# Issuing the decay rows of each head pair from another engine's queue

## The chip, the cores and the metric

The program runs on one core of one Trainium2 chip. The metric is the device time of one execution in microseconds. A core has five engines that matter here: TensorE (PE, matrix products), VectorE (DVE), ScalarE (ACT), GpSimd (POOL) and SyncE (SP). Each works through a queue of its own in a fixed order, and an instruction that waits holds back everything behind it in that queue. DMA transfers are started from a queue (here SP's or POOL's) and then run beside the engines.

## The reference

Causal attention with forget gates, then a dense layer with squared ReLU, then a mixture of eight experts of which each token takes two. The attention, cut to its core (4 batches, 8 heads, 576 positions, head size 64):

```python
scores = scale * np.matmul(q, k.transpose(0, 1, 3, 2))
log_f = np.log(np.clip(f, 0.0001, 1.0))
cum = np.cumsum(log_f, axis=-1)
decay = cum[:, :, :, None] - cum[:, :, None, :]
scores = np.where(causal, -1000000000.0, scores + decay)
attn = np.exp(scores - max); attn /= attn.sum + 1e-09
x = attn @ v                       # 2304 tokens x 512
x = np.maximum(x @ w_in, 0) ** 2 @ w_out
out = sum over a token's top-2 experts e of weight * relu(x @ w1[e]) @ w2[e]
```

## The kernel before, in words

All products run on PE in half precision, each operand split into a high and a low half, so a product is three matmuls.

Attention of the first 256 query rows of each batch ("head" part) runs first. The remaining 320 rows are 48 *units* (b, i, p): batch b, block of 128 queries i = 2, 3, 4, head pair p. `att_tick` (from L801) takes the units one after the other and mixes them with the steps of the dense layer. The stations of a unit:

- `att_s` (L213 to L230) makes its scores on PE in two PSUM tiles `ps`.
- `att_exp` (L242 to L252): DVE takes the row maximum, ACT the exponential.
- `att_split` (L265 to L278): ACT and DVE split the result into two halves (`phl`, or `ph4` for i = 4), and one DMA transpose issued on SP brings it into `pt`.
- `att_pv` (L307, L310), three ticks later: PE multiplies `pt` with the values `vs` into `po`.

Between them PE has the dense layer: `mm1` (L483, tile `m1`, 12 matmuls of 384 columns) and `mm2` (L527, tiles `acc`, 9 matmuls of 512 columns).

The decay needs no product of its own. `prep(b, p)` loads keys and queries of a pair into `setk<p>` and `setq<p>` (KK, QQ): ACT copies at L184 and L185, DVE's low halves at L186 and L187, and then L189 copies six rows of the cumulative log gates, kept in the tile `c16`, by DMA into partitions 64 to 69 of KK's plane 0. The matmuls L214 and L226, 70 partitions deep, read them there. L189 waits for L186, which still reads that plane. `prep(b+1, p)` belongs to the tick of the unit (b, 4, p), so the four copies of a batch are written ahead of the batch's first scores. Behind L189 in SP's queue stand the load of the next pair (L90), weight loads (L455) and the transposes of the units (L267, L278).

POOL has little to do in this stage: small memsets of `ph4` (L272) and of zeros (L585), and the six scatters of each routed chunk (L668, `table`), which wait for DVE's `si` (L665).

The order on every engine is set by a scheduler that, while the program is built, plays the program forward with its own estimates of durations, and puts each instruction where it becomes ready in that play. The source fixes which work exists and what depends on what; it doesn't fix the place of a matmul on PE.

Of the kernel before, what the change touches and what calls it, by code (L numbers as in the profile page):

```python
# [18 lines left out]
B, H, S, D = 4, 8, 576, 64  # L19
# [33 lines left out]
def attn_moe_moe_kernel(ctx: ExitStack, tc, qka, qk, v, f, w_io, wgn, noise, w1, w2, out):  # L53
    nc = tc.nc
# [24 lines left out]
    c16 = apool.tile([96, S], F16, name="c16")  # L79
# [82 lines left out]
    KK, QQ, VS = {}, {}, {}  # L162

    def make_set(n):
        KK[n] = apool.tile([128, 2, 2, S], F16, name=f"setk{n}", tag=f"setk{n}", bufs=1)
        QQ[n] = apool.tile([128, 2, 2, REST], F16, name=f"setq{n}", tag=f"setq{n}", bufs=1)
        q2 = QQ[n][64:70, 1]
        nc.gpsimd.memset(q2, -8.0)
        nc.gpsimd.affine_select(q2[:, 0], q2[:, 0], [[0, REST]], ALU.is_ge, 0.0, base=2, channel_multiplier=-1)
        nc.gpsimd.affine_select(q2[:, 1], q2[:, 1], [[0, REST]], ALU.is_ge, 0.0, base=-3, channel_multiplier=1)  # L170
# [6 lines left out]
    def prep(b, p):  # L177
        n = p
        if b == 0:
            make_set(n)  # L180
        t = raw.pop(("qk", b, p))
        k_ = t[:, 0:2 * S].rearrange("p (z s) -> p z s", z=2)
        q_ = t[:, 2 * S:SK].rearrange("p (z s) -> p z s", z=2)
        nc.scalar.activation(KK[n][:, 0], k_, AF.Copy)  # L184
        nc.scalar.activation(QQ[n][:, 0], q_, AF.Copy, scale=-1.0)  # L185
        nc.vector.scalar_tensor_tensor(KK[n][:, 1], KK[n][:, 0], half, k_, op0=ALU.mult, op1=ALU.subtract)  # L186
        nc.vector.tensor_tensor(QQ[n][0:64, 1], q_[0:64], QQ[n][0:64, 0], op=ALU.add)  # L187
        h0 = 8 * b + 2 * p
        nc.sync.dma_start(KK[n][64:70, 0], c16[3 * h0:3 * h0 + 6, None, :].to_broadcast([6, 2, S]))  # L189

    def prep_v(b, p):
        v_ = raw.pop(("v", b, p))
# [608 lines left out]
    def att_tick(k, pool_of):  # L801
        if k == 0:
            prep(0, 0)
            prep_v(0, 0)
            load_qk(0, 2)
            load_v(0, 2)
        if k < 3:
            prep(0, k + 1)
            prep_v(0, k + 1)
            if k == 0:  # L810
                load_qk(0, 3)
                load_v(0, 3)
            elif k == 1:
                load_qk(1, 0)
        if k < NU:
            u = units[k]
            att_s(u, pool_of(k))
            att_exp(u)
            b, i, p = u
            if i == 4 and b + 1 < B:  # L820
                prep(b + 1, p)
                if p < 3:
                    load_qk(b + 1, p + 1)
                elif b + 2 < B:
                    load_qk(b + 2, 0)
                if p > 1:
                    load_v(b + 1, p - 2)
            if i == NB and b:
                prep_v(b, p)
                if p < 2:  # L830
                    load_v(b, p + 2)
# [225 lines left out]
```

## Time and profile before

| | |
|---|---|
| median of 3 runs | 1033.73 us (1032.12 to 1035.33) |
| the profiled execution's own time | 1035.69 us |
| its span, first to last instruction | 1034.0 us |
| PE busy | 948.4 us, 92% of the span |
| DVE, ACT, POOL busy | 57%, 44%, 18% of the span |
| mean granted clock of TensorE | 0.959 of full speed |

A busy share is an average over stages. The units run from about 100 to 520 us, the experts fill the time from about 580 us to the end. What an edit in the attention is worth is read from the idle time of PE in that stretch and from what ended it.

### The profile page before, as it was taken

Reading aid. Unit: us, or ns where it says so; the run is one execution under the profiler, and the core shown is the slowest. Engines: PE = TensorE matmul, PEld = TensorE weight load, DVE = VectorE, ACT = ScalarE, POOL = GpSimd, SP = SyncE. Lnnn points to the kernel's source line nnn. Section 1 sums busy time; section 2 is a strip of 40 time slices with the busy share of each in tenths; the row PEclk is TensorE's granted clock in tenths of the full one; section 3 lists DMA queues with packets and bytes.
Section 4 is the critical chain, followed back from the end, with each engine's and each line's share of the span. In section 5 each row is a group of like instructions: output and inputs, shape, how many; then the busy total and the mean of one; then the engine's idle time right before and its main releaser. Section 6 shows DMA issues by size and latency. Waiting matters only on the chain.

```text
span 1034.0 us, 17720 instructions
## 1 busy us (share of the span) xinstructions
PE 948.4 (92%) x6850; PEld 534.5 (52%) x6850; DVE 590.5 (57%) x1325; ACT 456.4 (44%) x1005; POOL 181.5 (18%) x202
## 2 busy tenths in 40 slices
PE   2667899999889998999999899999899999999996
PEld 1554455455445554555544444466556565656562
DVE  7978989947668776776568242254534343432221
ACT  3875776756647655755455120134423232321010
POOL 8000000002020011002000404333231313120202
PEclk9558999999899998999999999999999999999999
DMA  7889898874977957973387542559994748350303
GB/s 257 243 197 247 221 237 210 209 188 64 196 146 180 255 134 108 200 134 72 62 255 240 127 98 27 97 75 291 293 192 116 196 118 229 82 122 2 51 3 49
DMA packets 240681, 160.92 MB, mean 156 GB/s; under 512 B 194163, under 2 KB 204915, under 8 KB 240595
## 3 DMA queue, kind: packets, MB, share of 16 engines
q1 hardware_dynamic: 230482, 138.75, 55.4%
q0 software_dynamic: 10112, 21.02, 10.7%
q8 instruction: 54, 0.88, 0.4%
q14 instruction: 33, 0.26, 0.1%
HBM read 88.97 MB, written 24.30 MB: 110 GB/s over the span
## 4 chain that ended last, share of the span: by engine, by line
PE 59%; DMA 10%; DVE 2%; issue 2%; SPq 1%; ACT 1%; POOL 1%; POOLq 0%; DVEq 0%
PE e L780 19%; PE e L767 17%; PE m L483 9%; PE acc L527 9%; DMA pt<-phl 4%; DMA wr<-in_w_dram 3%; PE po L307 1%; PE po L310 1%; DMA pt<-ph 1%; DMA xg<-x2d,tix 1%; PE ps L213 1%; PE ps L214 1%; DMA xgT<-xg 1%; DVE w2s L704 1%; DMA out_dram<-y,tix 0%
## 5 line engine op out<-in xcount | busy, mean ns | idle before, releaser
L767 PE MATMUL e<-xgT,w1s 128*128 128x320 f16 (+2 forms) x1536 | 218.1, 303 | 8.4 <-DMA xgT<-xg 4.6
L483 PE MATMUL m<-xT,win 128*128 128x384 f16 x1152 | 208.9, 331 | 4.8 <-ACT r L487 2.8
L780 PE MATMUL e<-w2s,hT 128*128 128x512 f16 x960 | 211.2, 379 | 1.9 <-ACT hT L771 1.7
L527 PE MATMUL acc<-wout,g 128*128 128x512 f16 x864 | 207.0, 381 | 4.8 <-DVE g L491 2.1
L767 PEld LDWEIGHTS <-w1s 128*128 128x128 f16 x1536 | 143.7, 99 | 81.6 <-issue 12.5
L483 PEld LDWEIGHTS <-win 128*128 128x128 f16 x1152 | 110.2, 99 | 83.1 <-issue 12.2
L780 PEld LDWEIGHTS <-hT 128*128 128x128 f16 x960 | 93.5, 98 | 111.7 <-ACT hT L771 2.1
L771 ACT ACTIVATE hT<-e 128x320 f16<-128x320 f32 (+2 forms) x128 | 54.1, 436 | 184.1 <-PE e L767 184.0
L527 PEld LDWEIGHTS <-g 128*128 128x128 f16 x864 | 80.8, 98 | 90.1 <-issue 2.4
L772 DVE SCALAR_TENSOR_TENSOR hT<-e,hT 128x320 f16<-128x320 f32 (+2 forms) x128 | 60.4, 487 | 96.0 <-ACT hT L771 95.8
L783 DVE TENSOR_SCALAR y<-e,gs 128x512 f32<-128x512 f32 x40 | 30.0, 749 | 144.9 <-PE e L780 134.0
L487 ACT ACTIVATE r<-m 128x384 f32<-128x384 f32 x96 | 46.8, 488 | 113.5 <-PE m L483 103.6
L784 POOL DMA_INDIRECT out_dram<-y,tix x40 | 63.1, 1576 | 144.6 <-DVE y L783 136.7
L703 ACT ACTIVATE w2s<-wr 128x1024 f16<-128x1024 f32 x32 | 32.5, 1050 | 104.4 <-PE e L780 88.5
L668 POOL DMA_INDIRECT table<-ent,si x36 | 37.8, 1049 | 230.5 <-DVE si L665 221.3
L242 DVE TENSOR_REDUCE sm<-ps 128x1 f32<-128x384 f32 (+2 forms) x96 | 53.1, 562 | 35.3 <-PE ps L230 16.1
L733 POOL DMA_INDIRECT xg<-x2d,tix x40 | 42.3, 1057 | 115.0 <-DMA xgT<-xg 102.1
L493 DVE TENSOR_TENSOR r<-r 128x384 f32<-128x384 f32 x64 | 35.3, 552 | 42.9 <-ACT g L488 42.8
L245 ACT ACTIVATE pr<-ps,sm 128x384 f32<-128x384 f32 (+1 forms) x64 | 40.0, 628 | 25.7 <-DVE sm L244 24.8
L488 ACT ACTIVATE g<-r 128x384 f16<-128x384 f32 x96 | 50.2, 523 | 1.7
L374 PE MATMUL psab<-hs 64*128 64x128 f16 (+1 forms) x192 | 28.0, 335 | 22.9 <-ACT pr L398 11.6
L704 DVE SCALAR_TENSOR_TENSOR w2s<-wr,w2s 128x1024 f16<-128x1024 f32 x32 | 38.0, 1220 | 15.4 <-ACT w2s L703 15.4
(264 smaller groups left out, 1071.2 us busy)
## 6 DMA issues: line engine op xcount, KB each, us to landing
wr<-in_w_dram SPq DMA_DIRECT2D x64, 512.0 KB
w<-in_w_io_dram SPq DMA_DIRECT2D x32, 512.0 KB
qkr<-in_qk_dram SPq DMA_DIRECT2D x16, 896.0 KB
vr<-in_v_dram SPq DMA_DIRECT2D x16, 320.0 KB
x2d<-x SPq DMA_DIRECT2D x18, 256.0 KB
qkh<-in_qka_dram SPq DMA_DIRECT2D x8, 512.0 KB
out_dram<-zero SPq DMA_DIRECT2D x5, 768.0 KB
vh<-in_v_dram SPq DMA_DIRECT2D x8, 256.0 KB
```

The lines of the kernel that those rows point to most:

```text
L242: seen[u] = nc.vector.tensor_reduce(sm[:, z:z + 1], ps[z][:, :N], AX.X, ALU.max).ins
L483: nc.tensor.matmul(ps, win[i][:, cc, wi, :], xT[:, xi, cc, r0:r0 + CH], start=(x == 0), stop=(x == 11))
L487: nc.scalar.activation(r, ps, AF.Relu)
L488: nc.scalar.activation(g[:, 0, :], r, AF.Square, scale=2.0 ** -10)
L527: nc.tensor.matmul(acc[t], g[:, gi, 128 * t:128 * t + 128], wout[i][:, wi, :], start=(i in ends[c][0] and x == 0), stop=(i in ends[c][1] a ...
L704: nc.vector.scalar_tensor_tensor(lo, t_, sc, hi, op0=ALU.mult, op1=ALU.subtract)
L733: nc.gpsimd.indirect_dma_start(out=xg, out_offset=None, in_=x2d[0:seen, :], in_offset=bass.IndirectOffsetOnAxis(ap=tix[:, j, 0:1], axis=0))
L767: nc.tensor.matmul(ps[:, :hw], w1s[:, cc, wi, 128 * i:128 * i + 128], xgT[:, 4 * xi + cc, hw * q:hw * q + hw], start=(x == 0), stop=(x == 11))
L771: nc.scalar.activation(hi, ps[:, :hw], AF.Relu)
L772: nc.vector.scalar_tensor_tensor(hT[:, i, 1, hw * q:hw * q + hw], ps[:, :hw], 0.0, hi, op0=ALU.max, op1=ALU.subtract)
L780: nc.tensor.matmul(ps, hT[:, i, hi, 128 * j:128 * j + 128], w2s[:, i, wi, :], start=(i == 0 and x == 0), stop=(i == NFE - 1 and x == 2))
L784: s_ = nc.gpsimd.indirect_dma_start(out=out, out_offset=bass.IndirectOffsetOnAxis(ap=tix[:, j, 0:1], axis=0), in_=y, in_offset=None, compu ...
```

## The change

The DMA of the six decay rows is issued on GpSimd's queue. Its source, destination and size stay. It happens 16 times (4 batches, 4 pairs).

```diff
         h0 = 8 * b + 2 * p
-        nc.sync.dma_start(KK[n][64:70, 0], c16[3 * h0:3 * h0 + 6, None, :].to_broadcast([6, 2, S]))
+        nc.gpsimd.dma_start(KK[n][64:70, 0], c16[3 * h0:3 * h0 + 6, None, :].to_broadcast([6, 2, S]))
```

Since the scheduler plays the program anew, the other engines' orders change too, from the tail of the head part up to the first scores of batch 3; behind that PE has the order that it had.

POOL's queue around the copies for batch 1 (`setk_1601` is pair 0, `setk_1618`, `setk_1743` and `setk_1869` are pairs 1 to 3; `ph_3011` and `ph_3106` belong to the units (0,4,2) and (0,4,3)); lines with + are new:

```order
 L272 MEMSET ph_3011 128x2x64
+L189 DMA setk_1601<-c_87 6x2x576
 L272 MEMSET ph_3106 128x2x64
+L189 DMA setk_1618<-c_87 6x2x576
 L668 DMA table<-ent,si 18432x2 x6
+L189 DMA setk_1743<-c_87 6x2x576
+L189 DMA setk_1869<-c_87 6x2x576
 L585 MEMSET zero 128x1024 x2
```

The copies of pairs 2 and 3 now stand behind the six scatters of the first routed chunk.

PE, before, directly ahead of the first matmul that reads `pt_5024`, the transposed tile of the unit (2,3,1) (`ps_5191` are scores of the unit (2,4,0)):

```order
L527 MATMUL acc2_4652<-wout7_189,g_5070 128x512
L224 LDWEIGHTS setq0_1602
L224 MATMUL ps_5191<-setk0_1601,setq0_1602 64x288
L226 LDWEIGHTS setq0_1602
L226 MATMUL ps_5191<-setk0_1601,setq0_1602 64x288
L307 LDWEIGHTS pt_5024
L307 MATMUL po_5107<-vs_4440,pt_5024 128x64
```

PE, now, at the same place:

```order
L230 LDWEIGHTS identw_97
L230 MATMUL ps_5192<-maskw_98,identw_97 64x64
L483 LDWEIGHTS win9_175
L483 MATMUL m1_5163<-xT_165,win9_175 128x384
L307 LDWEIGHTS pt_5024
L307 MATMUL po_5107<-vs_4440,pt_5024 128x64
```

(In both, rows that repeat are left out.) The whole of the scores of (2,4,0) and the twelve matmuls of the next `m1` now come first. Counted from the last score matmul of (2,3,1) to the first matmul on `pt_5024`, PE had 98 matmuls, of them 24 of L483, 24 of L527 and 34 of L307; now it has 124, of them 44, 27 and 30, and the remaining scores of (2,4,0).

PE, before, at the scores of the unit (0,4,3), whose two halves are `ps_2981` and `ps_2982`:

```order
L527 MATMUL acc2_2594<-wout13_195,g_2967 128x512
L224 MATMUL ps_2981<-setk3_1869,setq3_1870 64x288
L226 MATMUL ps_2981<-setk3_1869,setq3_1870 64x288
L224 MATMUL ps_2982<-setk3_1869,setq3_1870 64x288
L226 MATMUL ps_2982<-setk3_1869,setq3_1870 64x288
L230 MATMUL ps_2982<-maskw_98,identw_97 64x64
```

PE, now:

```order
L224 MATMUL ps_2981<-setk3_1869,setq3_1870 64x288
L226 MATMUL ps_2981<-setk3_1869,setq3_1870 64x288
L310 MATMUL po_3018<-vs_1628,pt_2913 64x64
L527 MATMUL acc0_2586<-wout13_195,g_2967 128x512
L527 MATMUL acc2_2594<-wout13_195,g_2967 128x512
L483 MATMUL m1_3143<-xT_165,win15_181 128x384
L527 MATMUL acc0_2586<-wout14_196,g_3063 128x512
L224 MATMUL ps_2982<-setk3_1869,setq3_1870 64x288
L226 MATMUL ps_2982<-setk3_1869,setq3_1870 64x288
L230 MATMUL ps_2982<-maskw_98,identw_97 64x64
```

(Weight loads and repeated rows are left out.) The second half of the scores has moved behind two blocks of the dense layer, while the first matmul that reads this unit's `pt_3105` stands at the same place of PE's queue as before: from the last score to it there were 96 matmuls, of them 36 of L483 and 18 of L527; now there are 78, of them 24 and 12.

## Rows read from the trace of the kernel before

**Rows 1.** The page, busy time by engine

```profile
PE 948.4 (92%) x6850; PEld 534.5 (52%) x6850; DVE 590.5 (57%) x1325; ACT 456.4 (44%) x1005; POOL 181.5 (18%) x202
```

**Rows 2.** Busy time by window: from:to, length, engines, clock, DMA share, GB/s

```profile
100.00:520.00 420.00, 397.92 (x3399) 219.36 (x3399) 310.12 (x803) 258.72 (x608) 38.09 (x51) 0.98 0.75 163
240.00:255.00 15.00, 14.69 (x92) 7.51 (x90) 11.77 (x33) 12.69 (x30) 6.70 (x6) 1.00 0.57 94
264.00:268.00 4.00, 4.00 (x41) 2.22 (x38) 2.52 (x7) 1.25 (x4) 0.00 (x0) 0.50 0.58 112
398.00:404.00 6.00, 6.00 (x43) 2.94 (x41) 0.69 (x2) 1.61 (x4) 0.41 (x2) 0.65 0.25 57
```

**Rows 3.** Waits of PE from 100 to 520 us: total, times, longest

```profile
PE po L307 <- DMA pt<-phl: 11.4, 6, 4.8
PE po L310 <- DMA pt<-ph: 4.6, 3, 3.6
```

**Rows 4.** Timeline of PE, its stalls: start, duration, instruction, [idle before, releaser]

```profile
191.89 0.87 PE L307 MATMUL po<-vs,pt 128*128 128x64 f16 x24 [0.98 <-DMA pt<-phl]
...
255.35 0.25 PE L310 MATMUL po<-vs,pt 128*64 128x64 f16 x4 [0.67 <-DMA pt<-ph]
...
263.81 0.58 PE L310 MATMUL po<-vs,pt 128*64 128x64 f16 x14 [3.60 <-DMA pt<-ph]
...
290.84 0.49 PE L307 MATMUL po<-vs,pt 128*128 128x64 f16 x11 [1.11 <-DMA pt<-phl]
...
307.67 0.20 PE L307 MATMUL po<-vs,pt 128*128 128x64 f16 x1 [2.33 <-DMA pt<-phl]
...
397.56 0.50 PE L307 MATMUL po<-vs,pt 128*128 128x64 f16 x6 [4.77 <-DMA pt<-phl]
```

**Rows 5.** Timeline of PE, last score matmuls of (0,4,2), (0,4,3), (2,3,1)

```profile
242.05 0.22 PE L230 MATMUL ps<-maskw,identw 64*64 64x64 bf16 x2
...
246.84 0.22 PE L230 MATMUL ps<-maskw,identw 64*64 64x64 bf16 x2
...
380.16 0.22 PE L215 MATMUL ps<-maskw,identw 128*128 128x128 bf16 x1
```

**Rows 6.** The moved line: times are ns, min/median/max

```profile
L189 SPq DMA_DIRECT2D setk<-c x16: 763/776/1206, 88.7 to 427.2; - x16
```

**Rows 7.** Timeline of SP's queue, issues

```profile
245.39 0.78 SPq L189 DMA_DIRECT2D setk<-c  x1
...
254.14 1.40 SPq L278 DMA_TRANSPOSE pt<-ph  x1
...
387.05 11.30 SPq L267 DMA_TRANSPOSE pt<-phl  x3
```

**Rows 8.** Timeline of DVE

```profile
249.40 1.40 DVE L186 SCALAR_TENSOR_TENSOR setk<-setk,half,qkr 128x1152 f16<-128x1152 f16 x1
...
253.21 0.86 DVE L277 TENSOR_TENSOR ph<-pr,ph 128x512 f16<-128x512 f32 x2 [0.50 <-ACT ph L276]
...
386.29 0.69 DVE L266 TENSOR_TENSOR phl<-pr,phl 128x512 f16<-128x512 f32 x1 [0.50 <-ACT phl L265]
```

**Rows 9.** POOL's scatters, all 36 (ns), and the last of the first six

```profile
L668 POOL DMA_INDIRECT table<-ent,si x36: 966/972/1619, 246.0 to 633.5; - x36
...
DMA to landing us min/median/max: 2.4/4.4/10.8
...
253.22 0.97 POOL L668 DMA_INDIRECT table<-ent,si  x1 [0.30 <-issue]
```

**Rows 10.** Timeline of PE, first matmul of batch 1 on pair 2's rows

```profile
264.62 0.53 PE L214 MATMUL ps<-setk,setq 70*128 70x384 f16 x1
```

**Rows 11.** The chain in order of time: blocks of the dense layer at full clock

```profile
310.75 1.95 PE m L483 x12
...
313.28 1.94 PE acc L527 x9
```

## The prediction

> **What bounds the kernel now.** I read the page first: PE is busy for 92% of the span, no other engine for more than 57% [rows 1]. So an edit is worth what it does to PE's idle time, and to the clock that PE gets. Then the windows: from 100 to 520 us, where the attention units run, PE is idle for 420.00 - 397.92 = 22.1 us [rows 2]. That is the most that this stretch can give back, apart from the clock. Then the waits of PE in it: 16.0 us in 9 waits end with the landing of a transposed tile `pt` that `att_pv` needs [rows 3]. The timeline has the six that matter here one by one [rows 4]; the two longest are 4.77 us (unit (2,3,1)) and 3.60 us (unit (0,4,3)). Both are followed by a stretch at the lower of TensorE's two levels: the granted clock is 0.50 in 264 to 268 us and 0.65 in 398 to 404 us [rows 2]. With PE busy throughout, that is another 4 x 0.50 = 2.0 us and 6 x 0.35 = 2.1 us of work lost. I count such a loss behind these two alone.
>
> So what counts is a race: after its scores a unit goes through DVE, ACT, DVE, a transpose and a landing, while PE works through whatever stands in its queue before that unit's `pt`. Where the queue is shorter than the chain, PE stands.
>
> **The change part by part.**
>
> *Removed from SP.* 16 issues of 0.776 us at the median [rows 6], 12.4 us of SP's queue. It would help PE only where a late transpose was late because of L189. At the two long stalls it wasn't: the transpose of (0,4,3) was issued at 254.14, right behind the end of DVE's split at 253.21 + 0.86 = 254.07, and that of (2,3,1) at 387.05, behind 386.29 + 0.69 = 386.98 [rows 7, 8]. The L189 at 245.39 [rows 7] was long done. I take 0 for the relief; the upper bound is 0.8 us for each of the other four stalls of [rows 4], 3.1 us.
>
> *Added to POOL.* 16 DMA issues with 12 short rows each. The trace of before shows none of this kind there; the nearest rows are the scatters, 0.966 to 1.619 us each, landing after 2.4 to 10.8 us [rows 9]. By them 15.5 to 25.9 us are added to an engine that is busy for 38.09 of 420 us in this stretch [rows 2]. What counts is where they stand. In batch 1 the copies for pairs 2 and 3 stand behind six scatters, of which the last ended at 253.22 + 0.97 = 254.19 [rows 9]. A copy of 0.966 and a landing of 4.4 us put pair 2's rows at 259.6; PE first read them at 264.62 [rows 10]. So 5 us are in hand and I take 0. The bounds are below, in the rival of the late rows. Behind the copies in POOL's queue stand memsets for units whose transposes come later; 0 too.
>
> A rule of the Trainium skill speaks against this move: "SBUF — State Buffer", section "SBUF: two separate sides", says that a DMA issued from GpSimd can't have its descriptors written while VectorE holds the port that the two share, and advises the other queue. Here six scatters ran while DVE was busy for 11.77 of 15 us [rows 2], and over all 36 none took more than 1.619 us [rows 9]: if that is the lock, it costs at most 0.65 us an issue on an engine with idle time, and the sum stays as it is.
>
> *Moved on PE.* The scheduler's new order is the larger part. I price a block of 12 matmuls of L483 at 1.95 us and 9 of L527 at 1.94 us [rows 11], so 0.163 and 0.216 us a matmul, and one of L307 at 0.87/24 = 0.036 us [rows 4].
>
> - Unit (2,3,1). Its last score matmul ended at 380.16 + 0.22 = 380.38 [rows 5], its tile was there at 397.56 [rows 4]: the chain took 17.2 us, of which PE worked 12.4 and stood 4.77. In the new order 20 matmuls of L483 (3.25 us), 3 of L527 (0.65) and the remaining scores of (2,4,0) (some 0.5) are added in between, and 4 of L307 (0.15) fall out: 12.4 + 4.25 = 16.7 us. A chain of 17.2 us leaves 0.5 us of stall, and the half-clock stretch goes with the rest: -(4.27 + 2.1) = -6.4 us. What is late next is (2,3,2); see the rivals.
> - Units (0,4,2) and (0,4,3). Before, the second's chain took 263.81 - 247.06 = 16.8 us and the first's 255.35 - 242.27 = 13.1 us [rows 4, 5]. Of the 16.8 us PE stood 3.60 + 0.67 = 4.3 and worked 12.5. The new order takes 12 matmuls of L483 and 6 of L527 out, 3.2 us: 9.3 us are left to cover a chain between 13.1 and 16.8 us. The stalls become 3.8 to 7.5 us, a change of -0.5 to +3.2; I take the middle, +1.4. The half clock behind it stays.
> - Unit (0,3,3), stall 0.98 us [rows 4]: between its last score and its `pt` 162 matmuls become 228, which covers it: -1.0 us.
> - Unit (1,2,3), stall 1.11 us [rows 4]: 144 matmuls become 162, the 18 more all of L307, 0.65 us: -0.6 us.
> - Unit (1,3,1), stall 2.33 us [rows 4]: 98 become 91, but with 9 more of L527 and 8 fewer of L483, to within some 0.1 us the same work: 0.
> - Units that lose cover without having stood before: (1,3,2) loses 18 matmuls (2.5 us of work), (1,4,2) and (2,3,3) some 4 us each. Their chains had 13.1 to 17.2 us in the longest and shortest cases above, and they keep 13 to 16 us. Bounds 0 and 4 us together; I take +1.2.
>
> Sum: -6.4 - 1.0 - 0.6 + 1.4 + 1.2 = -5.4 us. Against the profiled execution's 1035.69 us (span 1034.0) that is 1030.3 us; that execution lies 2.0 us above the median of the runs shown, 1033.73, so for the median I say 1028.3 us. With the best end of each term (all four remaining gains and the relief of SP) it is about -12, with the worst ends of the three last terms and nothing else lost about +1.
>
> **The rivals.**
>
> *The stall moves one unit on (no change).* PE comes to (2,3,2) 4.8 us earlier than before. SP issued the transposes of (2,3,1), (2,3,2) and (2,3,3) in one piece of 11.30 us from 387.05 on [rows 7]: each waits for the one ahead. If (2,3,2)'s tile doesn't come earlier, PE gives back most of the 4.27 us there, and a stall of that length brings the half clock back (2.1 us). For it: the three came in a row. Against it: in the new order the second score half of (2,3,2) stands earlier, right behind the first, and PE's work up to its tile is longer by about 1 us. Then the sum is -5.4 + 6.4 = +1.0, so 1034.7 us.
>
> *The decay rows come late (slower).* The place is POOL's queue in batches 1 to 3, pairs 2 and 3, behind the scatters (batch 1) or the zero memsets (batches 2 and 3). Price: with two copies of 1.619 us behind 254.19 and a landing of 10.8 us [rows 9] the rows are there at 268.2, 3.6 us after PE's L214 at 264.62 [rows 10], and each microsecond by which DVE's `si` comes later adds one. A stall of that length cost the half clock as well, 2.1 us [rows 2]: 5.7 us a batch. It decides as soon as the rows land after PE's arrival; it makes the kernel slower once two batches are hit: -5.4 + 2 x 5.7 = +6.0, so 1039.7 us. For it: the wait for `si` now stands ahead of rows that PE needs. Against it: 5 us in hand at the median landing, and PE itself has to wait for (0,4,3) ahead of those scores. The rule cited above would make just this longer.
>
> *SP's relief shows (more gain).* If transposes behind L189 really come 0.8 us earlier and (0,4,3)'s chain is the short one, the sum goes to about -5.4 - 3.1 - 1.9 = -10.4: 1023.3 us.
>
> **How the numbers follow.** The forecast gets 0.49, the stall that moves on 0.22, the late rows 0.12, the larger gain 0.09; 0.08 is left for new stalls in the reordered part that I haven't found, 0.07 of it slower and 0.01 no change. A change under 0.3%, 3.1 us, can't be told from none with these runs. The forecast's own range is 1025 to 1032 us, from the bounds of its terms without the half clocks; 0.04 of it lies above 1030.6 and counts as no change. Together: faster 0.49 - 0.04 + 0.09 = 0.54, same 0.22 + 0.04 + 0.01 = 0.27, slower 0.12 + 0.07 = 0.19. The range goes from 1022, below the larger gain, to 1037 us; it leaves out most of the slower cases, and some 0.05 at the lower end.
>
> **What would show each step.** At (2,3,1) the trace of after should show a stall under 1 us and no clock below 1.0 behind it; a stall over 2 us at that unit or the next makes the main term wrong. At (0,4,3) the stall should be 3.8 to 7.5 us together with (0,4,2), with a clock near 0.5 after it; the stall of (0,3,3) should be gone. L189 should stand on POOL with about 1 us an issue, and no L214 or L226 should wait for a DMA into `setk`; if one does, the rival of the late rows holds. From batch 3's first scores on, both traces should differ by a constant. If PE's idle time in the units' stretch is as large as before, but the time isn't, the clock's share was mis-sized.

## The result and the profile after

The changed kernel takes 1022.36 us at the median (6 runs, 1017.67 to 1023.87), the kernel before 1034.68 us beside it (6 runs, 1032.12 to 1036.52): ratio 0.9876, 95% interval 0.9853 to 0.9900, so 12.3 us faster. The forecast was 5.4 us faster. The sign was right and the time lies in the range, but the gain is more than double the forecast.

The page of the changed kernel, busy time by engine, which answers to [rows 1]:

```profile
PE 943.2 (92%) x6850; PEld 533.2 (52%) x6850; DVE 590.1 (58%) x1325; ACT 455.7 (45%) x1005; POOL 195.6 (19%) x218
```

Its windows: stretch, length, busy time of PE, PEld, DVE, ACT and POOL, then granted clock, DMA share and GB/s.

```profile
100.00:520.00 420.00, 405.58 (x3455) 224.16 (x3452) 315.52 (x811) 264.96 (x612) 47.88 (x65) 0.99 0.76 170
380.00:420.00 40.00, 39.12 (x358) 21.53 (x357) 31.87 (x73) 27.99 (x63) 8.81 (x14) 1.00 0.86 179
264.00:268.00 4.00, 4.00 (x19) 1.96 (x18) 4.00 (x10) 2.73 (x7) 0.00 (x0) 0.71 1.44 182
262.00:266.00 4.00, 3.78 (x39) 1.92 (x40) 2.16 (x5) 1.91 (x5) 0.00 (x0) 0.61 1.20 257
```

PE's idle time from 100 to 520 us fell from 22.1 us [rows 2] to 14.4. (The two windows don't hold quite the same work: a wait of 1.98 us for ACT at 515.86 us is in the changed kernel's, while its like before, 1.64 us at 527.85, is outside.) The half clock behind (2,3,1) is gone: 1.00 over 380 to 420 us, where before had 0.65 in 398 to 404 [rows 2]. Behind (0,4,3), whose stall now ends at 262.22 us, the clock still falls, to 0.61 in 262 to 266 us; in 264 to 268 us it is 0.71, where before had 0.50 [rows 2].

The changed kernel's waits of PE from 100 to 520 us for transposed tiles (total, times, longest), and two of its stalls in the timeline:

```profile
PE po L310 <- DMA pt<-ph: 3.7, 2, 3.5
...
PE po L307 <- DMA pt<-phl: 2.0, 1, 2.0
```

```profile
262.22 0.71 PE L310 MATMUL po<-vs,pt 128*64 128x64 f16 x26 [3.53 <-DMA pt<-ph]
...
305.27 0.47 PE L307 MATMUL po<-vs,pt 128*128 128x64 f16 x10 [1.96 <-DMA pt<-phl]
```

16.0 us of waits for tiles [rows 3] have become 5.7. Gone are the stalls of (0,3,3), (1,2,3) and (2,3,1), and that of 1.56 us at (3,3,1), for which the prediction had no term; (0,4,3) kept 3.53 of 3.60 us and (1,3,1) 1.96 of 2.33 [rows 4].

The moved line on GpSimd (ns, min/median/max):

```profile
L189 POOL DMA_DIRECT2D setk<-c x16: 544/572/827, 84.9 to 417.1; - x16
```

An issue costs 0.572 us, less than the 0.776 on SP [rows 6] and than the scatters of [rows 9] that served as its price. Its landing is not faster than priced: where the trace tells it (the changed kernel with its scatters later, below), it took 5.1 us at the median, against the 4.4 of [rows 9]. No instruction of PE waited for a DMA into `setk`.

To see where the time went, last score matmuls serve as marks, (0,4,3), (2,3,1) and (3,2,0) of the changed kernel, then (3,2,0) of the kernel before, whose other two are in [rows 5].

```profile
249.04 0.22 PE L230 MATMUL ps<-maskw,identw 64*64 64x64 bf16 x2
...
374.11 0.22 PE L215 MATMUL ps<-maskw,identw 128*128 128x128 bf16 x1
...
418.70 0.22 PE L215 MATMUL ps<-maskw,identw 128*128 128x128 bf16 x1
```

```profile
429.69 0.22 PE L215 MATMUL ps<-maskw,identw 128*128 128x128 bf16 x1
```

At (3,2,0) PE has done the same work in both orders, at (2,3,1) the new order has done 1.2 us less (by the prices of the prediction). So of the 13.1 us between the two spans, 380.38 - 374.33 - 1.2 = 4.9 us fell ahead of (2,3,1), (429.91 - 380.38) - (418.92 - 374.33) + 1.2 = 6.1 us from there to (3,2,0), and 2.1 us behind it.

### The profile page after: what moved, and what is told of

It reads as the page before. It is cut to its first block, busy times and chain, and to the rows that moved or that the text cites. A ratio compares the mean times of both kernels' runs of the same rounds, so it can differ in the third digit from the quotient of the medians.

```text
span 1020.9 us, 17749 instructions
## 1 busy us (share of the span) xinstructions
PE 943.2 (92%) x6850; PEld 533.2 (52%) x6850; DVE 590.1 (58%) x1325; ACT 455.7 (45%) x1005; POOL 195.6 (19%) x218
## 3 DMA queue, kind: packets, MB, share of 16 engines
q0 software_dynamic: 10624, 21.24, 10.9%
## 4 chain that ended last, share of the span: by engine, by line
PE 62%; DMA 12%; issue 10%; DVE 10%; POOL 2%; ACT 2%; SPq 1%; another core or an unknown queue 1%; POOLq 0%; DVEq 0%; ACTq 0%
PE e L780 19%; PE e L767 17%; PE acc L527 10%; PE m L483 10%; DMA w<-in_w_io_dram 2%; DMA wr<-in_w_dram 2%; DMA pth<-phlh 1%; DMA pt<-ph 1%; PE po L307 1%; DMA qkr<-in_qk_dram 1%; PE po L310 1%; DMA xg<-x2d,tix 1%; DVE sm L242 1%; DVE w L462 1%; DMA xgT<-xg 1%
## 5 line engine op out<-in xcount | busy, mean ns | idle before, releaser
L767 PE MATMUL e<-xgT,w1s 128*128 128x320 f16 (+2 forms) x1536 | 215.9, 301 | 8.6 <-DMA xgT<-xg 6.6
L483 PE MATMUL m<-xT,win 128*128 128x384 f16 x1152 | 206.9, 329 | 5.2 <-ACT r L487 3.6
L527 PE MATMUL acc<-wout,g 128*128 128x512 f16 x864 | 206.8, 381 | 3.8 <-DVE g L491 1.6
L483 PEld LDWEIGHTS <-win 128*128 128x128 f16 x1152 | 108.8, 99 | 80.5 <-issue 10.4
L527 PEld LDWEIGHTS <-g 128*128 128x128 f16 x864 | 81.2, 98 | 90.4 <-DVE g L491 2.3
L668 POOL DMA_INDIRECT table<-ent,si x36 | 38.1, 1057 | 205.9 <-DVE si L665 196.7
L733 POOL DMA_INDIRECT xg<-x2d,tix x40 | 46.1, 1153 | 112.7 <-DMA xgT<-xg 103.3
L242 DVE TENSOR_REDUCE sm<-ps 128x1 f32<-128x384 f32 (+2 forms) x96 | 53.4, 562 | 21.6 <-PE ps L215 12.4
L704 DVE SCALAR_TENSOR_TENSOR w2s<-wr,w2s 128x1024 f16<-128x1024 f32 x32 | 38.1, 1221 | 15.6 <-ACT w2s L703 15.5
```

Source lines behind the costliest of these rows:

```text
L242: seen[u] = nc.vector.tensor_reduce(sm[:, z:z + 1], ps[z][:, :N], AX.X, ALU.max).ins
L483: nc.tensor.matmul(ps, win[i][:, cc, wi, :], xT[:, xi, cc, r0:r0 + CH], start=(x == 0), stop=(x == 11))
L527: nc.tensor.matmul(acc[t], g[:, gi, 128 * t:128 * t + 128], wout[i][:, wi, :], start=(i in ends[c][0] and x == 0), stop=(i in ends[c][1] a ...
L733: nc.gpsimd.indirect_dma_start(out=xg, out_offset=None, in_=x2d[0:seen, :], in_offset=bass.IndirectOffsetOnAxis(ap=tix[:, j, 0:1], axis=0))
L767: nc.tensor.matmul(ps[:, :hw], w1s[:, cc, wi, 128 * i:128 * i + 128], xgT[:, 4 * xi + cc, hw * q:hw * q + hw], start=(x == 0), stop=(x == 11))
```

## The experiments

Theory T1: the scheduler's new order on PE, DVE and ACT made the gain. T2: SP's queue, freed of 16 issues, made it. T3: any shuffle moves the time, and parts of it don't add up. T4 and T5 came up on the way. The times of the kernel before differ by up to 5 us from one group of runs to another (medians of 1034.7 to 1039.4 us), so each run is read by its ratio to the runs of before beside it.

Several kernels hold an order fixed, whatever queue L189 is on. At the end of the program's main block they add edges of order, without waits:

```diff
+    traced = {i.name: i for i in nc.cur_bb.bb.instructions}
+    for steps_ in json.loads(zlib.decompress(base64.b85decode(ORDER))).values():
+        line_ = [f"I-{x}" for x in itertools.accumulate(steps_)]
+        for a_, b_ in zip(line_, line_[1:]):
+            tc.add_manual_dep(traced[b_], a_, mybir.DependencyInfo(mybir.DependencyClass.NoSync, mybir.DependencyReason.DATA), reason="order")
```

`ORDER` lists each engine's instructions as the kernel before or the changed one has them; L189 is left free where its queue isn't that order's.

**Order or queue.** The new order with `nc.sync` at L189:

> L189 is back on SP's queue, but PE, DVE, ACT and the rest of SP and POOL have the order of the changed kernel, held by order edges without waits. Theory T1 (the new order alone makes the gain): the time of the changed kernel, 1022.4 us, at most 1 us more; no stall at (2,3,1), none at (3,3,1). Theory T2 (the gain comes from SP's queue being freed of 16 issues): most of the gain is lost, 1031 to 1035 us. Mixed: the 1.56 us stall of (3,3,1) comes back because there the order had not changed, about 1024 us.

Measured: ratio 0.9872 (0.9846 to 0.9899), the whole gain without the move. The old order with `nc.gpsimd` at L189:

> L189 is issued on GpSimd as in the changed kernel, but all engines have the order of the kernel before, held by order edges without waits. T1: no gain, 1034 to 1035 us, the stalls of 4.77 us at (2,3,1) and 3.60 us at (0,4,3) as before. T2: the gain is there, 1022 to 1025 us. Mixed: only the stall of (3,3,1) goes, 1033 us.

Measured: 0.9975 (0.9952 to 0.9999), with the long stalls in place:

```profile
395.49 0.50 PE L307 MATMUL po<-vs,pt 128*128 128x64 f16 x6 [4.97 <-DMA pt<-phl]
```

T2 falls as the main cause: the queue alone is worth 2.6 us (0.1 to 5.0), the order alone all 12. (Even the 2.6 us are weak: moving batch 3's issues alone, below, gives nearly the same ratio with nothing in its trace to explain it.) The 1 us stall of (3,3,1) does go with the queue: 1.04 us in the first of these runs, 0.16 in the second.

**Which half.** The order changes at PE's place 2494 of 6850, old first and then the reverse; `nc.sync` in both:

> L189 on SP; every engine has the old order up to the second scores of batch 2 (344 us in the trace of before) and the new one from there. T1, additive: the traces give -3.8 us ahead of that place and -8.2 us behind it (4.77 stall and 2.1 clock at (2,3,1), 1.56 at (3,3,1)), so 1026.5 us. Rival T3 (any shuffle of the order changes the time, and the parts do not add up): a time between 1022 and 1037 that does not fit with the sum of this run's and the next run's gains being 12 us. T2: 1034.7 us.

> L189 on SP; every engine has the new order up to the second scores of batch 2 and the old one from there. T1, additive: -3.8 us, 1030.9 us, and the 4.77 us stall at (2,3,1) is still there with its half clock. T3: the sum of this gain and that of the run before misses 12 us by more than 3 us. T2: 1034.7 us.

Measured: 0.9950 (0.9927 to 0.9973) and 0.9935 (0.9912 to 0.9957), 5.2 and 6.7 us, together 11.9. The parts add up, against T3, but the first half is worth more than the traces had made me expect. In the second run the stall of (2,3,1) is back with 4.69 us.

**Six matmuls.** The smallest edit that closes the main stall by PE's order alone, on PE's queue:

```diff
 L226 MATMUL ps_5191<-setk0_1601,setq0_1602 64x288
-L307 MATMUL po_5107<-vs_4440,pt_5024 128x64 x6
 L527 MATMUL acc0_4644<-wout7_189,g_5070 128x512
...
 L230 MATMUL ps_5192<-maskw_98,identw_97 64x64
+L307 MATMUL po_5107<-vs_4440,pt_5024 128x64 x6
```

> L189 on SP and the whole old order, but the first six of the 24 matmuls on the tile pt of (2,3,1) stand 18 matmuls of the dense layer and half a unit's scores later on PE, right ahead of the other 18. That puts some 3.3 us of PE's work more between the unit's scores and its tile (12.7 to about 16 us, for a chain of 17.2). T1 (a unit's stall is chain minus PE's work ahead of its tile): the stall goes from 4.8 to about 1.2 us, its half clock goes, -5.4 us as in the second half of the new order: 1029 to 1031 us. Rival (the stall moves on to the next unit, whose transpose was issued in the same piece): 1034 us, with a stall of 3 to 4 us at (2,3,2).

Measured: 0.9970 (0.9945 to 0.9994), 3.1 us. The stall shrank to 1.97 us, yet the clock still fell:

```profile
402.98 0.87 PE L307 MATMUL po<-vs,pt 128*128 128x64 f16 x24 [1.97 <-DMA pt<-phl]
```

```profile
404.00:408.00 4.00, 4.00 (x16) 1.90 (x15) 0.64 (x1) 0.89 (x4) 0.20 (x1) 0.61 0.52 128
```

The direction fits T1, the size does not: in the new order the same stall is gone altogether.

**Two more orders**, made freely by the scheduler:

```diff
-        nc.sync.dma_start(KK[n][64:70, 0], ...
+        nc.scalar.dma_start(KK[n][64:70, 0], ...
```

> L189 is issued on ACT's queue in all batches, and the scheduler orders freely. SP is relieved just as by the change. In this order PE's work between scores and tile at (2,3,1) is 12.6 us, as before the change (17.0 in the changed kernel), at (0,3,3) 17.6 us as before, at (0,4,2) and (0,4,3) 9.3 and 11.1. T1: the stall of 4 to 5 us at (2,3,1) and its half clock stay, no more than a small gain, 1030 to 1036 us. T2 (SP's relief): 1022 to 1025 us.

```diff
-        nc.sync.dma_start(KK[n][64:70, 0], ...
+        (nc.gpsimd if b == 0 else nc.sync).dma_start(KK[n][64:70, 0], ...
```

> Only batch 0's four issues of L189 move to GpSimd; the scheduler orders freely. Its order has 29.9 us of PE's work at (0,3,3) as in the changed kernel, but 12.6 us at (2,3,1) as before. T1: the first part's gain of 4 to 5 us is there, the second's isn't: 1029 to 1031 us, and the stall of 4 to 5 us at (2,3,1) with its half clock stays. T2: a quarter of the gain, 1031.6 us or more, and no stall need stay.

Measured: 0.9931 (0.9906 to 0.9957) and 0.9869 (0.9843 to 0.9895), 7.2 and 13.6 us, both better than T1 expected when read by the ratio. The order with ACT's queue also has a stall of 3.85 us at (3,3,1), though L189 is off SP's queue there in all batches. These misses mattered most. With the old 12.6 us of PE's work ahead of the tile, (2,3,1) stood for 1.08 and 1.43 us instead of 4.77. So its chain itself was shorter, and the premise that it lasts 17.2 us was wrong. What differs is when SP issues the transpose, beside POOL's six scatters of L668. The kernel with batch 0 on GpSimd, the transpose, the first and last scatter, and the stall:

```profile
378.91 6.96 SPq L267 DMA_TRANSPOSE pt<-phl  x2
```

```profile
375.68 0.98 POOL L668 DMA_INDIRECT table<-ent,si  x1 [12.39 <-DVE si L665]
...
382.13 1.28 POOL L668 DMA_INDIRECT table<-ent,si  x1 [0.31 <-issue]
```

```profile
386.27 0.20 PE L307 MATMUL po<-vs,pt 128*128 128x64 f16 x1 [1.43 <-DMA pt<-phl]
```

The kernel before, POOL in the same place:

```profile
382.82 0.98 POOL L668 DMA_INDIRECT table<-ent,si  x1 [15.40 <-DVE si L665]
...
389.49 0.97 POOL L668 DMA_INDIRECT table<-ent,si  x1 [0.30 <-issue]
```

The changed kernel, SP and POOL; its last row waits for that same transpose, so it gives the landing:

```profile
379.06 1.86 SPq L267 DMA_TRANSPOSE pt<-phl  x1
```

```profile
377.60 1.06 POOL L668 DMA_INDIRECT table<-ent,si  x1 [12.78 <-DVE si L665]
...
385.92 0.20 POOL L272 MEMSET ph<- 128x128 f16 x1 [0.86 <-DMA pt<-phl]
```

Before, the transpose came 387.05 - 382.82 = 4.23 us after the first scatter [rows 7] and landed 10.5 us later, at 397.56 [rows 4]. With batch 0 on GpSimd it came 3.23 us after it and landed within 7.4; changed, 1.46 us after it and within 6.9. In all five runs that keep the old order and the scatters in this place (the kernel before, the old order on GpSimd, the run that begins with the new order, the six matmuls and, below, batch 3 alone) the distance was 4.2 us and the landing took 10.4 to 10.9. This gave theory T4: the scatters make the transposes late that come behind them. POOL's groups start at 246, 296, 383 and 475 us before the change, and (0,4,3), (1,3,1), (2,3,1) and (3,3,1) stand beside one each.

**Filling the new order's own stalls** (L189 on GpSimd, PE's queue alone changed):

```diff
-L310 MATMUL po_3018<-vs_1879,pt_3105 64x64 x30
 L213 MATMUL ps_3303<-setk2_1743,setq2_1744 128x384
...
 L527 MATMUL acc1_3392<-wout0_182,g_3243 128x512
+L310 MATMUL po_3018<-vs_1879,pt_3105 64x64 x30
...
-L307 MATMUL po_3851<-vs_3187,pt_3768 128x64 x10
 L224 MATMUL ps_3935<-setk0_1601,setq0_1602 64x288
...
 L230 MATMUL ps_3936<-maskw_98,identw_97 64x64
+L307 MATMUL po_3851<-vs_3187,pt_3768 128x64 x10
```

> The changed kernel with its own order, L189 on GpSimd, but on PE the 30 matmuls on the tile pt of (0,4,3) stand some 3.7 us of work later (behind the next unit's first scores, 12 matmuls of L483 and 6 of L527), and the first ten on that of (1,3,1) stand 12 matmuls of L483 and a unit's scores later, some 3 us. T1: the stalls of 3.53 and 1.96 us and about 1.2 us of lowered clock go, 1016 to 1018 us. Rival: what stands ahead now waits in its place (the accumulators of the next chunk, or the output of the row), 1021 us or more.

Measured: 1017.31 us, 0.9805 (0.9778 to 0.9832). Both stalls are gone, and three of 0.80 to 1.08 us came at units of batch 1. It beats both kernels.

**Without two groups of scatters:**

```diff
-        for t in range(NT):
+        for t in range(0 if c in (2, 3) else NT):
             for k in range(2):
                 s_ = nc.gpsimd.indirect_dma_start(
```

> The kernel before (L189 on SP, its own order on PE, ACT and SP) without the two groups of six scatters of L668 that start at 382.8 and 474.6 us; the entries of chunks 2 and 3 are left out of the table, so the experts miss those tokens. Theory T4 (the transpose of (2,3,1) was late because it was issued in the middle of the scatters and its writes stand behind theirs): from its issue to its landing some 7 us instead of 10.5, the stall at (2,3,1) 1 to 2 us instead of 4.77, its half clock gone, the stall of (3,3,1) gone; (0,4,3) and (1,3,1), whose scatters stay, as before: -5 to -8 us. T1 in its plain form (the chain is 17.2 us in itself and only PE's order decides): the stall stays at 4 to 5 us, less than 2 us are gained.

Measured: 0.9930 (0.9905 to 0.9955), 7.2 us. SP's issue for (2,3,1), and PE at its tile, with no wait:

```profile
387.42 3.03 SPq L267 DMA_TRANSPOSE pt<-phl  x1
```

```profile
393.10 0.35 PE L307 MATMUL po<-vs,pt 128*128 128x64 f16 x6
```

The order is the old one, the issue at the old time, but the tile is there within 5.7 us instead of 10.5, and neither a stall nor a lower clock is left. (3,3,1) doesn't stand either. (0,4,3) and (1,3,1), whose scatters stayed, stand for 3.67 and 2.27 us. T4 holds, and T1's plain form falls.

**Scatters later, nothing left out.** The old order on PE and ACT; on DVE four tiny copies, which release the scatters, move down their queue; one of the four:

```diff
-L665 CAST si<-sf 128x6
 L266 TENSOR_TENSOR phl<-pr,phl 128x4x128
...
 L242 TENSOR_REDUCE sm<-ps 128x1
+L665 CAST si<-sf 128x6
```

> L189 on SP and the old order on PE, ACT and SP; on DVE the four copies into si (L665) that release the scatters of chunks 0 to 3 stand some 22 instructions later, behind the row maxima of (1,2,1), (1,4,0), (2,4,0) and (3,4,0), whose tiles have 18 to 21 us of PE's work ahead of them. T4: the stalls at (0,4,3), (1,3,1), (2,3,1) and (3,3,1) (3.6, 2.3, 4.8, 1.6 us) fall below 2 us each, the half clocks with them: -6 to -11 us. Rival T5 (any transpose that meets the scatters is late, and PE stands there instead): no gain, stalls of 2 to 4 us at the units now beside the scatters.

> The version with the new order, L189 on GpSimd and the two tiles' matmuls moved back, with the same four copies into si later. T4: of its 3.5 us of stalls between 200 and 285 us one or two go, -1 to -3 us against that version (ratio to before 0.978 or less). T5: a new stall, ratio 0.981 or more.

Measured: 0.9849 (0.9815 to 0.9884) and 0.9807 (0.9779 to 0.9836). The first is 15.6 us (12.0 to 19.2) faster than before, with L189 on SP and PE's order untouched. Its waits of PE for tiles, and the clock where (0,4,3) used to cost it:

```profile
PE po L307 <- DMA pt<-phl: 4.9, 4, 1.8
...
PE po L310 <- DMA pt<-ph: 0.4, 1, 0.4
```

```profile
264.00:268.00 4.00, 4.00 (x36) 2.10 (x34) 2.54 (x6) 0.55 (x2) 0.24 (x1) 1.00 1.31 136
```

All four stalls are gone; the longest that are left are 1.84 us at (1,2,0) and 1.73 at (1,2,3). The second run is T5's: the small stalls went, and one of 3.33 us came at a unit of batch 1 beside the moved scatters, so nothing was gained over the filled order.

**Batch 3 alone on GpSimd** (`nc.gpsimd if b > 2 else nc.sync`):

> Only batch 3's four issues of L189 move to GpSimd; the order of PE, DVE and ACT is word for word that of the kernel before. T1: the time of before within 1.5 us. T2 in a small form (where L189 isn't in SP's queue, the tile of (3,3,1) lands 1 us earlier): -1 us, its stall of 1.0 to 1.6 us gone; the other stalls stay.

Measured: 0.9978 (0.9959 to 0.9996). The trace shows the old stalls, 4.87 us at (2,3,1) and 1.19 at (3,3,1). So batch 3's issues aren't what made (3,3,1) land 1 us earlier, and 2 us of this ratio have no place in the trace.

**How much is the order's own.** No scatters of chunks 0 to 3 (`range(NT if c > 3 else 0)`), in either kernel with its own order; and the changed kernel with the four copies later:

> The kernel before, its order on PE, DVE, ACT and SP unchanged, without the scatters of chunks 0 to 3 (their entries are left out of the table). T4: the stalls of (0,4,3), (1,3,1), (2,3,1) and (3,3,1) are all gone with their half clocks, about -15 us as with the scatters moved: ratio 0.983 to 0.987. If (0,4,3) and (1,3,1) had other causes, only the -7 us of the run without groups 2 and 3: 0.993.

> The changed kernel with its own order held by order edges, without the same scatters. T4 (nearly all that the new order gave was that it took transposes out of the scatters' way): without them the two orders lie 2 to 5 us apart, not 12, so ratio to before 0.979 to 0.983; what is left is the stalls at (0,3,3) and (1,2,3) and some in the head part. T1 alone: the 12 us between the orders stay, 0.972 or less.

> The changed kernel with its own order and with nothing left out; the four copies into si stand later on DVE, as in the old order's run of this kind. T4: within 5 us of that run (ratio 0.980 to 0.986), so that the change is worth little once the scatters are out of the way. T1: 12 us below it.

Measured: 1021.18, 1015.01 and 1020.26 us; 0.9836 (0.9811 to 0.9860), 0.9787 (0.9771 to 0.9804) and 0.9842 (0.9820 to 0.9865). Windows from 180 to 305 us, old order and new order without scatters; before and changed kernel had a clock of 0.97 and 0.99 there:

```profile
180.00:305.00 125.00, 120.93 (x993) 65.90 (x992) 93.42 (x263) 79.80 (x182) 2.52 (x5) 1.00 0.73 169
```

```profile
180.00:305.00 125.00, 123.89 (x1013) 67.41 (x1011) 91.73 (x262) 77.32 (x176) 6.27 (x13) 1.00 0.75 170
```

Without scatters the orders lie 5 to 6 us apart, not 12: by the ratios 0.0049, 5.1 us (some 2 to 8 by the two intervals), by the medians 6.2. PE's stalls of 0.5 us or more from 100 to 305 us tell the same: 9.3 us in the old order, 4.5 in the new. So, by the difference, about half of the change's gain is that the new order's transposes met the scatters less; the other half is the order's own. With the scatters moved, the changed kernel has the ratio of the old order treated the same way, 0.9842 and 0.9849: there the rest went into a new stall of 2.52 us beside the moved scatters and into the clock behind it, 0.50 in 270 to 276 us.

What (0,4,3) kept in the changed kernel is the scatters' too. Its transpose there, then its transpose and PE at its tile in the new order without scatters:

```profile
255.19 1.37 SPq L278 DMA_TRANSPOSE pt<-ph  x1
```

```profile
252.89 1.33 SPq L278 DMA_TRANSPOSE pt<-ph  x1
```

```profile
256.53 0.71 PE L310 MATMUL po<-vs,pt 128*64 128x64 f16 x26 [0.37 <-DMA pt<-ph]
```

From issue to tile it is 262.22 - 255.19 = 7.0 us with the scatters and 3.6 without, and the stall is 0.37 us instead of 3.53.

## Why the prediction was right in sign and short in size

- *Removed from SP: 0, bound 3.1.* The 2.6 us with the old order lie inside the bound, their interval (0.1 to 5.0) reaches past it; with the new order nothing is to be seen (0.9872 with SP, 0.9876 with GpSimd).
- *Added to POOL: 0.* Right, and the issue was cheaper than its price. The rival of the late rows is refuted. The rule cited from the Trainium skill ("SBUF — State Buffer", section "SBUF: two separate sides") shows no cost in the issue here: DVE was busy for 315.52 of 420 us, and none of the 16 issues took more than 0.827 us. Whether DVE held the shared port at any of them no row tells.
- *(2,3,1): -6.4.* The size held, 6.1 us up to (3,2,0); the reason was half of it. I took the chain of 17.2 us as given and let 4.25 us of added work cover it. More work alone gave 3.1 us (the six matmuls); taking the scatters away removed the whole stall without moving PE. In the new order both happen: the chain was 385.92 - 374.33 = 11.6 us there, which the old 12.4 us of work would have covered by itself. So it is partly luck that the size held. The trace that the prediction used had the evidence: 10.5 of the 17.2 us lay between issue and landing [rows 4, 7], and the six scatters stood in the rows of POOL beside it.
- *(0,4,2) and (0,4,3): +1.4.* This is the step that failed first. It took the chain from the lengths in one trace (13.1 to 16.8 us, of which it priced the middle), as if they held when the order changes, so that 3.2 us less of cover becomes stall. Measured: the cover shrank as forecast, to 9.3 us, yet 4.27 us of stalls became 3.70, with less of the half clock, since from its last score to its tile (0,4,3) took 262.22 - 249.26 = 13.0 us instead of 16.8. The last scatter ended 3.9 us ahead of its transpose there, while before the last one ran beside the issue. Single traces scatter: the two stalls come to 3.2 to 5.2 us in the six traces that keep the old order and the scatters here, and to 2.5 to 4.3 in three of the new order.
- *(0,3,3): -1.0.* Right: it stays in the old order without scatters (1.39 us) and goes with the new one. *(1,2,3): -0.6.* Right in kind, 1.1 us measured.
- *(1,3,1): 0.* Right here (2.33 to 1.96), though the stall is the scatters' and goes with them; in the two runs with the new order here and L189 on SP it was 0.28 and 0.40.
- *Units that lose cover: +1.2.* None of them stood. They kept 13 to 16 us of work, so their chains in the new order were no longer than that; the loss was priced, again, with chains of the old order.
- *The traces differ by a constant from batch 3 on.* No: the 1.56 us stall of (3,3,1) went, in the changed kernel and in the old order with all 16 issues on GpSimd (0.16 us), while the new order on SP kept 1.04. Batch 3's issues alone don't do it, and with all 16 on ACT's queue, in another order, it stood for 3.85. Why its tile lands 1 us earlier is open.

The terms ahead of (2,3,1) came to about +0.6 us and measured -4.9: the two that were losses didn't happen, and one of them was a gain, since the length of a chain had been taken from one trace as a constant. Eleven stalls of 0.5 us or more from 100 us to (2,3,1), 15.5 us in all, became five with 10.5 us; five of the eleven lie ahead of 142 us, where the head part ends, and had no term (5.5 us, in the changed kernel two with 3.9).

One sum of the prediction is loose: with the worst ends named and the other terms as priced, its list gives -0.8 us, not the +1 that it states.

Of the rivals, the stall that moves one unit on didn't come: nothing waits for the tile of (2,3,2). Its ground was a misreading: the piece of 11.30 us in [rows 7] is three rows merged, and the transposes of (2,3,2) and (2,3,3) were each issued right behind their own split on DVE (391.81 and 395.43 us), not behind the one ahead.

```profile
391.89 1.87 SPq L267 DMA_TRANSPOSE pt<-phl  x1
...
395.50 2.86 SPq L267 DMA_TRANSPOSE pt<-phl  x1
```

```profile
391.12 0.69 DVE L266 TENSOR_TENSOR phl<-pr,phl 128x512 f16<-128x512 f32 x1 [0.63 <-ACT phl L265]
...
394.74 0.69 DVE L266 TENSOR_TENSOR phl<-pr,phl 128x512 f16<-128x512 f32 x1
```

The time is that of the rival of SP's relief (1023.3), but not for its reason, as the two pinned runs show.

## What to carry to other kernels

A stall's length is the chain minus the work ahead of it, and both can change with the order: before a chain is used as a constant, its longest link should be compared with the same link at units that don't stand. Where that link is a transfer, the other queues' transfers in the same microseconds are the first suspects; here four copies of 0.16 us, put later on DVE, were worth at least about as much as the change itself (15.6 us, 12.0 to 19.2, against 12.3, 10.3 to 15.2). When a one-line change reshuffles a schedule, the two orders pinned on either queue tell in two runs which of them the time belongs to.

## What the runs showed of the hardware that was not expected

- Six small scatters of a router's chunk, issued on GpSimd's queue, delay a transpose issued on SP's. (2,3,1)'s, issued 4.2 us behind the first of them in the old order, took 10.4 to 10.9 us to landing, against 5.7 or less without them. Issued 1.5 us behind it in the new order it took 6.9, against 376.73 - 370.49 = 6.2 or less without them. The distance alone doesn't set the delay: before the change (0,4,3)'s, issued 254.14 - 245.97 = 8.2 us behind the first, took 9.7 us to PE.
- The traces tell only a part of where the time goes. While (2,3,1)'s transpose was under way before the change, the DMA queues moved next to nothing from 389.1 to 391.6 us (22 packets from 389 to 391); without the scatters a like pause lasted from 389.4 to 390.6 us (27 packets). What makes the pause, and what the rest of the delay is, stays open.
- The granted clock fell to 0.61 behind a stall of only 1.97 us, but with two stalls of 2.71 and 1.54 us, at 256 and 262 us of the run that begins with the new order, it stayed at 1.00 from 250 to 268 us.
- A DMA of twelve short rows took 0.572 us to issue on GpSimd and 0.776 on SP.
